# Strassen products for query and key, and PSUM banks of their own for turned tiles, in a kernel of retention, channel MLP and mixture of attention experts

## The chip, the cores and the metric

The kernel runs on one core of a Trainium2 chip. The metric is the device time of one execution in microseconds (us), the median of several runs. Matmuls run on TensorE (PE; its loads of weights are listed as PEld), elementwise work on VectorE (DVE), ScalarE (ACT) and GpSimd (POOL); SyncE (SP) issues all transfers. All inputs and outputs are fp32, and matmuls of large operands are made from a rounded high part and a low part (three matmuls: high x high, high x low, low x high).

## The reference, cut to what matters

```python
# 1 retention: B=2, H=8, S=768, D=64
for t in range(S):
    state = gamma * state + einsum('bhd,bhe->bhde', k[:, :, t], v[:, :, t])
    y[:, :, t] = scale * einsum('bhd,bhde->bhe', q[:, :, t], state)
x = y as [B, S, 512]
# 2 channel MLP, d = 512, inner 2048
xn = (x - mean) / sqrt(var + 1e-6) * g_ln
x = x + maximum(xn @ w_ch1, 0) @ w_ch2
# 3 mixture of 4 attention experts, head size 64, the best 2 of each token
logits = x @ w_gate ; w = softmax of the two best
for e in range(4):
    q, k, v = x @ wq[e], x @ wk[e], x @ wv[e]
    a = softmax(causal(q @ k.T / 8))
    out += w[e] * (a @ v @ wo[e])     # where e is among the two best
```

## The kernel before, in words

The work is written down as steps (`P.add`): each names the engines that may do it with a planned cost, the buffers that it reads and writes, and a priority (its place in the program, a bias, and a rank from the table `RANK`, which is kept by step name). `Plan.issue` then runs a simulation in Python: whenever an engine is free it takes the ready step of the lowest priority whose buffers find a place, and the order found is the order in which the instructions are issued. At run time every engine works through its own list in that order; a planned time that is not kept turns into a wait. Loads are planned at 372 GB/s and a latency of 2.2 us, and all go through SP's queue in order.

SBUF is one arena with places given by kind (`PL`), PSUM is eight banks of 512 words. Turned tiles (transposes on PE) go to places of kind `pb` (in the retention) and `pc` (in the attention). A turned tile has two halves, one for each half of the partitions, and `two` puts them at the same columns of two neighbouring banks; two such tiles of 256 columns share a pair of banks. The planner takes them for independent.

Stage 1, `r_tile`, 12 times (6 chunks of 128 tokens x 2 batches): keys and queries (`kq`) and values and keys (`vk`) are loaded, four and three buffers; scores (L581), masking (DVE L587), the chunk's own part (L610), the part from the state (L600), the update of the state (L618); then the tile is turned (`turn`, L422, xT into t1), normalized (statistics L642 to L644, L650, L651, xn at L655), turned back (xn into t2), copied (xc, L664) and split into a high and a low part, XH and XL.

Stage 2 is the MLP in eight slices f of 256 inner columns. Weights arrive in pieces (`load_piece`, `split_piece` on ACT, POOL and DVE). For f = 0 and 1 the first product is plain (`m_h`, L766). For the other six it is a Strassen scheme of seven products in place of eight (`m_h7`, L858) with sums of tokens (`x_sums`, POOL, once per batch) and of weights (`w_sums`). The second product, `m_c` (L788), is added to the running state XT by DVE; for f = 7 the sum is split again into XH and XL (L798, L801, L804). XT itself is not kept then.

Stage 3: `q_proj` makes queries and keys of one token half and one half of the columns with 12 matmuls (L952); `q_val` makes values and gate logits (L976); `a_scores` makes scores, softmax and scaling by the gate (L1047, L1054, L1062, L1068, L1069, L1076); `a_turn` turns the probabilities in parts of up to four blocks (L422) and copies them out on ACT or DVE (`COPY`, L446); `a_value` (L1117) and `a_out` (L1144) follow. Batch 1's projections are mixed with batch 0's attention. The groups of two query tiles are taken in the order 1, 2, 0 in batch 0 and 0, 1, 2 in batch 1. At the start some matmuls on constants (L529) keep PE at work until data is there.

Of the kernel before, what the change touches and what calls it, by code (L numbers as in the profile page):

```python
# [19 lines left out]
try:  # L20
# [15 lines left out]
E, HD = 4, 64  # L36
# [12 lines left out]
SWITCH = 0.125  # L49
LAST = 10000  # L50
FILL = 12
TWO = ("pb", "pc")
# [6 lines left out]
WORDS = 205 * KB  # L59
QUEUES = {"ps1": "s", "ps2": "s", "pr": "pr", "pt": "pt", "ptn": "pt", "sm": "sm", "at": "at", "w": "w", "h": "h", "raw": "raw", "wy": "wy",  # L60
          "w1": "w1", "S": "S", "t": "t", "u": "u", "sf": "sf",
          "am": "am", "vs": "vs", "xn": "xn", "xc": "xc"}
ROUNDED = {"x", "w", "w1", "S", "t", "h", "wq", "wk", "wv", "wo", "qk0", "qk1", "at"}


class Buf:
# [1249 lines left out]
```

## Time and profile before

| | us |
|---|---|
| median of 3 runs (442.19 to 445.38) | 442.72 |
| the profiled execution | 442.45 |
| its span in the trace | 440.7 |
| busy: PE, PEld | 429.4, 402.4 |
| busy: DVE, ACT, POOL | 309.8, 217.7, 212.0 |
| share of PE in the chain that ended last | 90% |

The span runs from the first to the last instruction of the trace. Busy time of an engine is the union of its instructions. The chain that ended last is followed back from the last instruction, at each step to what released it. The idle time before a group is given with the releasers, the instructions whose end let it start.

### The profile page before, as it was taken

The numbers are of one execution on the slowest core, as the hardware profiler recorded it, in microseconds if no ns is written. First come the engines' busy times: TensorE is split into PE (matmuls) and PEld (weight loads), VectorE is DVE, ScalarE is ACT, GpSimd is POOL, SyncE is SP. The second block draws the span as 40 slices with busy tenths as digits, with TensorE's granted clock in tenths as the row PEclk, the third lists the DMA queues.
The fourth block names the chain that finished last, engine by engine and source line by source line (L and its number), as shares of the span: only waits on it lengthen the run. The fifth ranks groups of instructions, "written<-read, shape, count | busy, mean of one in ns | idle before, by whom it ended". The sixth has DMA issues, their size and how long they took to land.

```text
span 440.7 us, 9076 instructions
## 1 busy us (share of the span) xinstructions
PE 429.4 (97%) x3546; PEld 402.4 (91%) x3546; DVE 309.8 (70%) x743; ACT 217.7 (49%) x460; POOL 212.0 (48%) x219
## 2 busy tenths in 40 slices
PE   9988999999999999999999999999999999999996
PEld 8877889999999999999999999999999877887765
DVE  2769978765778876868877655668556778667663
ACT  1568775342656346335353264234533666656552
POOL 2668865999999528117136054200401343422430
PEclk9999999999999999999999999999999999999999
DMA  8999432210322304104112002001100001001121
GB/s 288 328 337 345 133 109 84 97 49 1 106 86 92 101 0 143 50 1 136 54 59 88 1 1 96 1 0 55 48 1 1 1 12 39 2 0 49 50 97 49
DMA packets 11995, 35.18 MB, mean 80 GB/s; under 512 B 1840, under 2 KB 2480, under 8 KB 11952
## 3 DMA queue, kind: packets, MB, share of 16 engines
q1 hardware_dynamic: 11952, 34.60, 22.7%
q8 instruction: 28, 0.46, 0.4%
q14 instruction: 15, 0.12, 0.1%
HBM read 31.45 MB, written 3.15 MB: 79 GB/s over the span
## 4 chain that ended last, share of the span: by engine, by line
PE 90%; ACT 3%; DVE 2%; DMA 2%; POOL 1%; issue 1%; SPq 0%; POOLq 0%; DVEq 0%
PE ps L788 30%; PE ps L858 20%; PE ps L766 8%; PE ps L952 8%; PE ps L1117 4%; PE ps L976 4%; PE ps L422 4%; PE ps L1144 4%; PE ps L1047 3%; DMA raw<-in_w_dram 2%; PE ps L529 2%; PE ps L610 1%; PE ps L581 1%; ACT xn L655 1%; PE ps L600 1%
## 5 line engine op out<-in xcount | busy, mean ns | idle before, releaser
L788 PE MATMUL ps<-h,w 128*128 128x384 f32 x768 | 142.4, 335 | 0.0
L788 PEld LDWEIGHTS ps<-h,w 128*128 128x128 f32 x768 | 133.7, 188 | 0.7 <-DVE ps L798 0.3
L794 DVE TENSOR_TENSOR xT<-xT,ps 128x384 f32<-128x384 f32 x112 | 60.2, 550 | 30.6 <-PE ps L788 30.1
L1076 POOL TENSOR_SCALAR pr<-pr,sm,gate 128x384 f32<-128x384 f32 (+5 forms) x48 | 34.0, 718 | 77.9 <-DVE sm L1069 34.1
L719 POOL TENSOR_TENSOR w<-wy,w 128x512 fp32r<-128x512 f32 x26 | 34.0, 1319 | 38.1 <-PE ps L788 23.4
L858 PE MATMUL ps<-t,S 128*128 128x384 f32 x216 | 42.1, 334 | 0.0
L858 PEld LDWEIGHTS ps<-t,S 128*128 128x128 f32 x216 | 37.8, 188 | 0.0
L1062 ACT ACTIVATE pr<-pr,sm 128x384 f32<-128x384 f32 (+5 forms) x48 | 31.7, 663 | 9.9 <-DVE sm L1054 9.9
L766 PE MATMUL ps<-x,w 128*128 128x384 f32 x192 | 35.2, 337 | 0.0
L877 ACT ACTIVATE h<-ps 128x384 fp32r<-128x384 f32 x36 | 17.7, 490 | 32.9 <-PE ps L788 20.6
L766 PEld LDWEIGHTS ps<-x,w 128*128 128x128 f32 x192 | 33.2, 188 | 0.3
L685 ACT ACTIVATE wx<-raw 128x512 f32<-128x512 f32 x32 | 21.5, 671 | 23.8 <-DVE ps L692 16.0
L687 POOL TENSOR_SCALAR wx<-wx 128x512 f32<-128x512 f32 x32 | 20.0, 625 | 23.9 <-ACT wx L685 23.0
L867 ACT ACTIVATE u<-ps 128x384 f32<-128x384 f32 x36 | 17.5, 488 | 25.3 <-PE ps L858 16.6
L858 PE MATMUL ps<-x,w 128*128 128x384 f32 x144 | 28.6, 334 | 0.0
L689 DVE TENSOR_SCALAR ps<-wx 128x512 uint32<-128x512 uint32 x32 | 22.0, 688 | 6.4 <-POOL wx L687 6.1
L858 PEld LDWEIGHTS ps<-x,w 128*128 128x128 f32 x144 | 25.3, 188 | 0.0
L1054 DVE CUSTOM_DVE_ANT_0 pr<-ps,mask 128x384 f32<-128x384 f32 (+4 forms) x48 | 22.1, 495 | 3.2 <-PE ps L1047 2.2
L695 DVE SCALAR_TENSOR_TENSOR wy<-raw,ps 128x512 uint32<-128x512 uint32 x32 | 21.8, 683 | 2.3 <-POOL w L719 1.7
L879 DVE SCALAR_TENSOR_TENSOR h<-ps,h 128x384 fp32r<-128x384 f32 x36 | 19.4, 551 | 5.3 <-ACT h L877 5.2
L692 DVE SCALAR_TENSOR_TENSOR ps<-wx,ps 128x512 uint32<-128x512 uint32 x32 | 22.2, 695 | 1.1
L587 DVE TENSOR_TENSOR am<-ps,caus 128x512 f32<-128x512 f32 x24 | 15.5, 683 | 9.9 <-PE ps L581 9.9
(122 smaller groups left out, 822.7 us busy)
## 6 DMA issues: line engine op xcount, KB each, us to landing
raw<-in_w_dram SPq DMA_DIRECT2D x32, 512.0 KB, 3.4
kq<-in_kq_dram SPq DMA_DIRECT2D x11, 512.0 KB, 5.1
vk<-in_vk_dram SPq DMA_DIRECT2D x9, 512.0 KB, 5.5
out_dram<-ob SPq DMA_DIRECT2D x11, 256.0 KB, 2.0
vk<-in_vk_dram SPq DMA_DIRECT2D x4, 256.0 KB, 3.8
vraw<-in_wv_dram SPq DMA_DIRECT2D x1, 520.0 KB, 3.9
kq<-in_kq_dram SPq DMA_DIRECT2D x2, 256.0 KB, 5.2
mraw<-in_wk_dram SPq DMA_DIRECT2D x1, 512.0 KB, 4.6
```

The source lines that it names most:

```text
L689: DVE(0.69, lambda: dve.tensor_scalar(u32(z), u32(x), 4, 1, op0=OP.logical_shift_left, op1=OP.logical_shift_right), r=[x], w=[z])
L692: DVE(0.7, lambda: dve.scalar_tensor_tensor(u32(z), u32(x), 0x80000000, u32(z), op0=OP.bitwise_and, op1=OP.bitwise_or), r=[x, z], w=[z])
L695: DVE(0.7, lambda: dve.scalar_tensor_tensor(u32(y), words(0), 29, u32(z), op0=OP.logical_shift_right, op1=OP.bitwise_or), r=[raw, z], w=[y])
L719: POOL(1.3, lambda: pool.tensor_tensor(f32r(l), f32(y), f32(h), OP.subtract), r=[y, h], w=[l])
L766: pe.matmul(f32(pa, TB), lhsT=wt, rhs=blk(f32r(xt[b][j]))[:, k], start=(n == 0), stop=(n == 11))
L788: pe.matmul(f32(pa, TB), lhsT=wt, rhs=t, start=(n == 0), stop=(n == 5))
L794: DVE(0.55, lambda: dve.tensor_tensor(blk(f32(xt))[:, k], blk(f32(xt))[:, k], f32(pa, TB), OP.add), r=[pa] + [(xt, cc, w) for cc in range( ...
L858: pe.matmul(f32(pa, TB), lhsT=wt, rhs=t, start=(first and n == 0), stop=(n == 5), skip_group_check=True)
L952: pe.matmul(f32(pa, TB), lhsT=mw(n, lo, k, p * 128, (p + 1) * 128), rhs=blk(f32r(xt))[:, k], start=(i == 0), stop=(i == 11))
L1054: DVE(0.22 + wide * 1.04e-3, lambda ks=ks, n=n, z=z, SC=SC: dve.tensor_tensor_reduce(f32(PR[z])[:, ks], f32(SC[z])[:, :wide], f32(MASK)[:, ...
L1062: ACT(act_c(nk) + .18, lambda pr=pr, z=z: act.activation(f32(pr, nk), f32(pr, nk), AF.Exp, bias=f32(sm)[:, z:z + 1], scale=-1.0, accum_out ...
L1076: POOL(0.34 + nk * 0.84e-3, lambda pr=pr, z=z, e=e: pool.tensor_scalar(f32(pr, nk), f32(pr, nk), f32(sm)[:, 6 + z:7 + z], GT[b, j][:, cc, ...
```

## The change

- Query and key projections: `q_proj` now takes a whole batch and one weight and makes seven products of six matmuls in place of eight. The sums of wk and wq are made when these are loaded (`load_mw` 4 to 6). The sums of tokens are made by a second `x_sums` per batch, from XT, which the last `m_c` now writes as well (`m_c` 5, an ACT copy). Value projections of a batch come ahead of its query and key projections.
- Turned tiles: each has a pair of banks of its own; three places for `pb`, four for `pc`. Scores and outputs may use every bank. The third group of a batch is turned in two parts of up to six blocks, not three of up to four, and the value product waits only for the parts that it reads.
- The sum c22 of `m_h7` goes to PSUM; the sums of weights are made by POOL alone.
- 14 KB more of SBUF for each partition: six places for `kq`, four for `vk`, and more for turned probabilities; `pr` has 11 places in place of 12.
- The planner: transfers at 335 GB/s; an engine is free for its next step 0.05 to 0.1 us ahead of a step's end (`LEAD`); the two batches' states count as one buffer. The table of ranks is new throughout and is left out here.

```diff
--- before.py
+++ after.py
...
+LEAD = {"V": 0.085, "A": 0.1, "G": 0.05}
...
-TWO = ("pb", "pc")
...
-WORDS = 205 * KB
+WORDS = 219 * KB
...
+        n.eng = {e: c - LEAD.get(e, 0.0) for e, c in eng.items()}
...
+        n.lat = lat + max(LEAD.get(e, 0.0) for e in eng)
...
+    PL["kq"] += region(o_z, 4 * KB, 2)
+    PL["vk"] += region(o_z + 8 * KB, 4 * KB, 1)
...
+    PL["Sq"] = region(o_z, 4 * KB, 2) + region(o_h + 28 * KB, 4 * KB, 2)
+    PL["uq"] = region(o_z + 8 * KB, 3 * KB // 2, 4)
...
-    PL["pr"] = region(o_xt, 3 * KB, 8) + region(o_h + 24 * KB, 3 * KB, 4)
...
+    PL["pr"] = region(o_xt, 3 * KB, 6) + region(o_r + 36 * KB, 3 * KB, 4) + region(o_h + 24 * KB, 3 * KB, 1)
...
-    PL["psa"] = banks[4:][::-1]
-    PL["ps1"] = banks[:4]
+    PL["psa"] = banks[::-1]
+    PL["ps1"] = banks
...
-    PL["pb"] = [("P", 1024 * i + 256 * k, 256) for i in (1, 2, 3) for k in range(2)]
-    PL["pc"] = [("P", 1024 * i + 256 * k, 256) for i in (3, 2) for k in range(2)]
...
-    def two(b):
-        i, k = divmod(b.at[1], 1024)
-        return ps[:, 1024 * i:1024 * i + 1024].rearrange("p (h c) -> p h c", h=2)[:, :, k:k + 256]
+    PL["pb"] = [("P", 1024 * i, 1024) for i in (1, 2, 3)]
+    PL["pc"] = [("P", 1024 * i, 1024) for i in (3, 2, 1, 0)]
...
-        P.add({"D": nbytes / 372e3 + 0.03}, lambda e: fn(), r, w, lat=2.2)
+        P.add({"D": nbytes / 335e3 + 0.03}, lambda e: fn(), r, w, lat=2.2)
...
-            PE(0.47, upd, form="columns", r=[(vk, 1), vs] + (["first"] if i == 1 else []), w=[(STATE, b)] + (["first"] if i == 0 else []))
+            PE(0.47, upd, form="columns", r=[(vk, 1), vs], w=[STATE])
...
-            P.add({"V": 1.5, "G": 0.76} if f < ALONE else {"G": 0.75}, lambda e, i=i, p=p, q=q, op=op: (dve if e == "V" else pool).tensor_tensor(
+            P.add({"G": 0.75}, lambda e, i=i, p=p, q=q, op=op: (dve if e == "V" else pool).tensor_tensor(
...
-        P.add({"V": 2.4, "G": 2.41} if f < ALONE else {"G": 2.5}, lambda e: (dve if e == "V" else pool).tensor_tensor(f32r(l), f32(t), f32(h), OP.subtract),
+        P.add({"G": 2.5}, lambda e: (dve if e == "V" else pool).tensor_tensor(f32r(l), f32(t), f32(h), OP.subtract),
...
+        ACT(0.49, lambda: act.activation(blk(f32(xt))[:, k], f32(pa, TB), AF.Copy), r=[pa], w=[(xt, "k", k)])
+        P.at = "m_c 6"
         DVE(0.55, lambda: dve.tensor_tensor(blk(f32r(xl))[:, k], f32(pa, TB), blk(f32(xh))[:, k], OP.subtract),
-            r=[pa, (xh, "k", k)], w=[(xl, "k", k)] + (keys(xl) if k == 0 else []))
...
+    def x_sums(b, own=True):
...
-        for t, kh, j in ((2, 0, 1), (0, 0, 0), (1, 1, 1), (3, 1, 0)):
+        for t, kh, j in ((2, 0, 1), (0, 0, 0), (1, 1, 1), (3, 1, 0)) if own else ():
...
-            both(lambda en, t=t, p=p, q=q: en.tensor_tensor(plain(tl[t]), plain(tl[p]), plain(tl[q]), OP.subtract),
-                 [tl[p], tl[q]], [tl[t]])
+            both(lambda en, t=t, xp=xp, xq=xq: en.tensor_tensor(plain(tl[t]), xp(), xq(), OP.subtract), rp + rq, [tl[t]])
...
-        c22 = new("u")
+        c22 = new("ps")
...
+        if n in ("wk", "wq"):
+            sh, sl = new("Sq"), new("Sq")
...
+            for i, p, q, op in ((0, lambda: at(0, 1), lambda: at(1, 1), OP.add),
+                                (1, lambda: part(0), lambda: at(0, 0), OP.subtract),
+                                (2, lambda: at(0, 0), lambda: at(0, 1), OP.subtract),
+                                (3, lambda: at(1, 0), lambda: part(1), OP.subtract)):
+                P.at = "load_mw 4"
+                POOL(0.76, lambda i=i, p=p, q=q, op=op: pool.tensor_tensor(part(i), p(), q(), op), r=[raw], w=[sl])
+            P.at = "load_mw 5"
+            ACT(1.1, lambda: act.activation(f32r(sh), plain(sl), AF.Copy), r=[sl], w=[sh])
+            P.at = "load_mw 6"
+            POOL(2.41, lambda: pool.tensor_tensor(f32r(sl), plain(sl), f32(sh), OP.subtract), r=[sl, sh], w=[sl])
+            MW[n, "S"] = (sh, sl)
...
-    def q_proj(b, j, n, p):
...
+    def q_proj(b, n):
+        sh, sl = MW[n, "S"]
...
+        def product(pa, wn, xn, first):
...
-            PE(1.06, mm, r=list(MW[n][:2]) + xkeys(xh) + xkeys(xl) + ["seven"], w=[pa])
...
+            PE(1.04, mm, r=[h, l] + xr + ["seven"], w=[pa])
...
+        def add(dst, pa, u):
+            P.at = "q_proj 3"
+            DVE(0.55, lambda: dve.tensor_tensor(f32(dst, TB), f32(pa, TB), f32(u), OP.add), r=[pa, u], w=[dst])
...
+        pa, pb, pc = (new("ps") for _ in range(3))
+        product(pa, "a0", "x00", True)
+        c1 = keep(pa)
+        product(pb, "s1", "t1", True)
+        add(pb, pb, c1)
+        product(pa, "y0", "x10", False)
+        out(pa, 0, 0)
+        u2 = keep(pb)
+        product(pc, "s0", "t0", True)
+        product(pb, "s2", "t2", False)
+        u3 = keep(pb)
+        c22 = new("ps")
+        add(c22, pc, u3)
+        product(pb, "y1", "t3", False)
+        out(pb, 1, 0)
+        product(pc, "s3", "x11", False)
+        add(pc, pc, u2)
+        out(pc, 0, 1)
+        out(c22, 1, 1)
...
+            for z in range(2):
+                dve.tensor_scalar(m[:, 4 + z:5 + z], m[:, 2 + z:3 + z], 1e-9, None, op0=OP.add)
...
-            for s0 in range(0, len(slots), 4):
-                part = slots[s0:s0 + 4]
+            half = (len(slots) + 1) // 2 if len(slots) > 4 else len(slots)
+            for s0 in range(0, len(slots), half):
+                part = slots[s0:s0 + half]
...
+        half = (0, 4, 6)[g]
+        needs = {j0: sorted({min((2 * j0 + i) // half, 1) if half else 0 for i in (0, 3)}) for j0 in range(0, nj, 2)}
...
+    x_sums(0, False)
     flush()
+    x_sums(1, False)
...
     def q_phase(b):
         q_alloc(b)
         for j in range(NB):
-            for n in ("wk", "wq"):
-                for p in range(2):
-                    q_proj(b, j, n, p)
-            P.bias += 20 * (b + 1)
             for t in range(TPB):
                 q_val(b, TPB * j + t)
             gates(b, j)
-            P.bias -= 20 * (b + 1)
+        for n in ("wk", "wq"):
+            q_proj(b, n)
...
```

## Rows read from the trace of the kernel before

**Rows 1.** Stages: span, busy us (instructions) of PE, PEld, DVE, ACT, POOL; clock, DMA, GB/s.

```profile
0.00:45.00 45.00, 40.05 (x700) 35.17 (x702) 29.55 (x72) 23.56 (x50) 25.86 (x38) 1.00 0.91 321
80.00:120.00 40.00, 40.00 (x233) 40.00 (x232) 26.94 (x45) 16.72 (x30) 39.75 (x29) 1.00 0.17 61
82.90:319.00 236.10, 236.10 (x1362) 235.67 (x1360) 169.47 (x305) 105.75 (x200) 123.80 (x101) 1.00 0.17 57
319.00:440.70 121.70, 115.38 (x1113) 96.66 (x1112) 79.80 (x302) 63.22 (x166) 33.99 (x48) 1.00 0.08 27
```

**Rows 2.** Chain of work that ended last: start us, us, what.

```profile
7.05 2.02 PE ps L581 x32
...
48.18 1.99 PE ps L581 x32
...
82.86 8.33 PE ps L788 x48
...
306.65 8.32 PE ps L952 x48
314.97 4.16 PE ps L788 x24
...
319.86 1.24 PE ps L788 x6
...
325.26 8.60 PE ps L976 x72
```

**Rows 3.** Groups of PE, 0 to 82.86 us: busy, mean ns | idle before, releasers.

```profile
L529 PE MATMUL ps<-negs 128*128 128x128 f32 x32 | 6.7, 396 | 1.1 <-DVE half L546 1.1
...
L422 PE MATMUL ps<-ident,xn 64*128 64x64 f32 x96 | 5.6, 231 | 1.2 <-ACT xc L664 0.6 <-DVE mv L642 0.4
L422 PE MATMUL ps<-ident,xT 64*128 64x64 f32 x96 | 5.2, 231 | 1.9 <-ACT xn L655 1.2 <-ACT xc L664 0.6
```

**Rows 4.** The same chain, one landing of weights.

```profile
20.52 7.56 DMA raw<-in_w_dram
```

**Rows 5.** Waits of SP's queue: us in total, times, longest.

```profile
SPq L505 <- PE ps L618: 12.8, 6, 3.7
```

**Rows 6.** Waits of all engines: us in total, times, longest.

```profile
DVE pt L446 <- ACT pt L446: 4.0, 8, 1.2
```

**Rows 7.** Groups of PE, 319 to 440.7 us.

```profile
L422 PE MATMUL ps<-ident,pr 64*128 64x64 f32 x336 | 15.8, 228 | 2.8 <-DVE pt L446 1.6 <-ACT ptn L446 0.7 <-DVE at L1131 0.3
```

**Rows 8.** The chain again, turns of 16 and 6.

```profile
371.74 0.66 PE ps L422 x16
...
425.87 0.33 PE ps L422 x6
```

**Rows 9.** Timeline of PE: start us, us, what.

```profile
20.01 0.46 PE L422 MATMUL ps<-ident,xT 64*128 64x64 f32 x8
20.31 0.41 PE L422 MATMUL ps<-ident,xn 64*128 64x64 f32 x8
...
34.74 0.41 PE L422 MATMUL ps<-ident,xT 64*128 64x64 f32 x8
```

**Rows 10.** Timeline of ACT.

```profile
21.69 0.60 ACT L664 ACTIVATE xc<-ps 128x512 f32<-128x512 f32 x1 [1.46 <-POOL vs L571]
...
23.05 0.78 ACT L655 ACTIVATE xn<-ps,mv 128x512 f32<-128x512 f32 x1
...
41.07 0.78 ACT L655 ACTIVATE xn<-ps,mv 128x512 f32<-128x512 f32 x1 [1.80 <-POOL mv L651]
```

**Rows 11.** Groups of POOL, shapes apart.

```profile
L821 POOL TENSOR_TENSOR t<-t,t 128x768 f32<-128x768 f32 x8 | 15.0, 1876 | 0.3
...
L735 POOL TENSOR_TENSOR sf<-wy 128x256 f32<-128x256 f32 x6 | 4.7, 778 | 0.0
...
L925 POOL TENSOR_TENSOR wv<-vraw,wv 128x1040 fp32r<-128x1040 f32 x1 | 2.4, 2443 | 0.1
```

**Rows 12.** Timeline of DVE.

```profile
307.17 1.94 DVE L804 TENSOR_TENSOR x<-ps,x 128x384 fp32r<-128x384 f32 x4
```

More of the change, by code (lines that the diff above doesn't have):

```diff
@@ L218, in fits @@
                 for o in live.get(sp, ()):
-                    if (o.users or o.end > t) and any(x < y + size and y < x + o.at[2] for x in strips(o.kind, o.at[1])
-                                                      for y in strips(b.kind, off)):
+                    if (o.users or o.end > t) and o.at[1] < off + size and off < o.at[1] + o.at[2]:
                         break
@@ L421, in turn @@
                 hs = slice(64 * h, 64 * h + 64)
-                pe.transpose(two(dst)[:, h, i * 64:i * 64 + 64], src(i)[hs], ident[hs, hs])
+                pe.transpose(two(dst, 64 * n)[:, h, i * 64:i * 64 + 64], src(i)[hs], ident[hs, hs])
     P = Plan()
@@ L818, in x_sums, with part @@
                  keys(XH[b][j]) + keys(XL[b][j]), [tl[t]])
-        for t, p, q in ((0, 2, 0), (2, 1, 2), (1, 1, 0), (3, 3, 1)):
+        xs = {2: (0, 1), 0: (0, 0), 1: (1, 1), 3: (1, 0)}
+        def part(t, new):
+            if own or new:
+                return lambda: plain(tl[t]), [tl[t]]
+            kh, j = xs[t]
+            return lambda: f32(XT[b][j])[:, kh * TW:(kh + 1) * TW], [(XT[b][j], "k", 2 * kh + k) for k in range(2)]
+        for t, p, q, made in ((0, 2, 0, ()), (2, 1, 2, ()), (1, 1, 0, (0,)), (3, 3, 1, (1,))):
+            (xp, rp), (xq, rq) = part(p, p in made), part(q, q in made)
             P.at = "x_sums 2"
-            both(lambda en, t=t, p=p, q=q: en.tensor_tensor(plain(tl[t]), plain(tl[p]), plain(tl[q]), OP.subtract),
-                 [tl[p], tl[q]], [tl[t]])
+            both(lambda en, t=t, xp=xp, xq=xq: en.tensor_tensor(plain(tl[t]), xp(), xq(), OP.subtract), rp + rq, [tl[t]])
         for t in range(4):
@@ L941, in q_alloc, with mm @@
             VV[b, t] = new(f"vv{b}")
-    def q_proj(b, j, n, p):
-        cs = slice(j * TB, (j + 1) * TB)
-        pa = new("ps")
-        xh, xl = XH[b][j], XL[b][j]
-        for hf in range(2):
-            def mm(hf=hf):
-                i = 6 * hf
-                for k in (2 * hf, 2 * hf + 1):
-                    for lo, xt in ((0, xh), (0, xl), (1, xh)):
-                        pe.matmul(f32(pa, TB), lhsT=mw(n, lo, k, p * 128, (p + 1) * 128), rhs=blk(f32r(xt))[:, k],
-                                  start=(i == 0), stop=(i == 11))
+    def q_proj(b, n):
+        sh, sl = MW[n, "S"]
+        def product(pa, wn, xn, first):
+            h, l = (sh, sl) if wn[0] == "s" else MW[n][:2]
+            c0, step = (256 * int(wn[1]), 128) if wn[0] == "s" else ((512 if wn[0] == "y" else 0) + 128 * int(wn[1]), 256)
+            if xn[0] == "t":
+                xs = TH[b][int(xn[1])], TL[b][int(xn[1])]
+                xr, xat = list(xs), lambda k: tuple(f32r(t)[:, k * TB:(k + 1) * TB] for t in xs)
+            else:
+                kh, xs = int(xn[1]), (XH[b][int(xn[2])], XL[b][int(xn[2])])
+                xr, xat = xkeys(xs[0]) + xkeys(xs[1]), lambda k: tuple(blk(f32r(t))[:, 2 * kh + k] for t in xs)
+            def mm():
+                i = 0
+                for k in range(2):
+                    wh, wl = (f32r(t)[:, c0 + k * step:c0 + k * step + 128] for t in (h, l))
+                    xh, xl = xat(k)
+                    for wt, t in ((wh, xh), (wh, xl), (wl, xh)):
+                        pe.matmul(f32(pa, TB), lhsT=wt, rhs=t, start=(first and i == 0), stop=(i == 5), skip_group_check=True)
@@ L954, in mm @@
                         i += 1
             P.at = "q_proj 1"
-            PE(1.06, mm, r=list(MW[n][:2]) + xkeys(xh) + xkeys(xl) + ["seven"], w=[pa])
-        hi, lo = (QK[n, y, b, p] for y in range(2))
-        by = 0.125 if n == "wq" else 1.0
-        P.at = "q_proj 2"
-        ACT(0.485, lambda: act.activation(f32r(hi)[:, cs], f32(pa, TB), AF.Copy, scale=by), r=[pa], w=[(hi, j)])
-        P.at = "q_proj 3"
-        DVE(0.556, lambda: dve.scalar_tensor_tensor(f32r(lo)[:, cs], f32(pa, TB), by, f32(hi)[:, cs], op0=OP.mult, op1=OP.subtract),
-            r=[pa, (hi, j)], w=[(lo, j)])
+            PE(1.04, mm, r=[h, l] + xr + ["seven"], w=[pa])
@@ new lines, in keep, with out @@
+        def keep(pa):
+            u = new("uq")
+            P.at = "q_proj 2"
+            ACT(0.49, lambda: act.activation(f32(u), f32(pa, TB), AF.Copy), r=[pa], w=[u])
+            return u
+        def add(dst, pa, u):
+            P.at = "q_proj 3"
+            DVE(0.55, lambda: dve.tensor_tensor(f32(dst, TB), f32(pa, TB), f32(u), OP.add), r=[pa, u], w=[dst])
+        def out(src, p, j):
+            cs = slice(j * TB, (j + 1) * TB)
+            hi, lo = (QK[n, y, b, p] for y in range(2))
+            by = 0.125 if n == "wq" else 1.0
+            P.at = "q_proj 4"
+            ACT(0.485, lambda: act.activation(f32r(hi)[:, cs], f32(src, TB), AF.Copy, scale=by), r=[src], w=[(hi, j)])
+            P.at = "q_proj 5"
+            DVE(0.556, lambda: dve.scalar_tensor_tensor(f32r(lo)[:, cs], f32(src, TB), by, f32(hi)[:, cs], op0=OP.mult, op1=OP.subtract),
+                r=[src, (hi, j)], w=[(lo, j)])
@@ L1099, in a_turn @@
                 COPY(n * C, lambda pt=pt, s0=s0, n=n: f32(pt)[:, s0 * C:(s0 + n) * C].rearrange("p (n h c) -> p h n c", n=n, h=2),
-                     lambda pa=pa, n=n: two(pa)[:, :, :n * 64].rearrange("p h (n c) -> p h n c", n=n),
-                     [pa], [(pt, s0 // 4)])
+                     lambda pa=pa, n=n: two(pa, n * 64).rearrange("p h (n c) -> p h n c", n=n),
+                     [pa], [(pt, s0 // half)])
         return PT
@@ L1122, in a_value @@
                 PE((0.87 if j0 + 2 < nj else 0.65) * len(zs) / 2, mm, form="columns",
-                   r=[VV[b, j0], VV[b, j0 + 1]] + [(pt, j0 // 2) for pt in (*PT, *also)], w=[av])
+                   r=[VV[b, j0], VV[b, j0 + 1]] + [(pt, i) for pt in (*PT, *also) for i in needs[j0]], w=[av])
             cs = slice(zs[0] * C, (zs[-1] + 1) * C)
```

38 lines of the change are left out of this document (19 added, 19 removed), and 148 rows, old and new, of the table RANK.

## Prediction

> **What bounds the kernel now.** I read the busy time by stage first, then the chain of work that ended last, then the idle time of TensorE (PE) by group, then the other engines where the change puts work. In [rows 1] PE is busy for all of 82.9 to 319 us, at a granted clock of 1.00; it has idle time only in the first 45 us and after 319. DVE, ACT and POOL have time left in each of these stages; POOL alone is full for one stretch, 39.75 of 40 us from 80 to 120. So between 82.9 and 319 nothing but fewer or shorter matmuls shortens the run. The chain gives their price: 48 matmuls of 384 columns take 8.33 us [rows 2], 0.1735 us each, 1.04 us for a product of six.
>
> PE's idle time is small and countable. In the first 45 us it is busy for 40.05 [rows 1], so 4.95 us are idle; 1.1 us of that is ahead of the filler matmuls of L529, which nothing can use because the first keys land at 7.05 [rows 2, 3]. Of the fillers' 6.7 us, 28 of 32 run before 7.05 and four (0.64 us) after. What can be won there is 4.95 - 1.1 + 0.64 = 4.5 us. After 319 PE is busy for 115.38 of 121.70 us [rows 1]; of the 6.3 idle 2.8 us lie in front of the turns of the probabilities at L422 [rows 7], and the other 3.5 I put behind the last matmul (last copy and store). That is all: 4.5 and 2.8 us of stalls, and the matmuls themselves.
>
> **The sum goes against the profiled execution**, 442.45 us (span 440.7 and 1.75 around it), which is 0.27 under the median of 442.72.
>
> **Strassen for query and key.** Before, each of two batches, two token halves, two weights and two column halves takes 12 matmuls, 192 in all. After, each batch and weight takes seven products of six, 2 x 2 x 7 x 6 = 168. The operands keep their shapes (128 x 128 weights, 384 columns), and the 48 matmuls of L952 in [rows 2] take 8.32 us, the same price as in the channel MLP. 24 x 0.1735 = 4.16 us leave PE, in a stretch where PE has no idle to swallow them. What is added lies on other engines: per weight four sums and a low part on POOL, per batch eight POOL operations of 1.88 us [rows 11] for the sums of tokens, with four ACT copies, 16 ACT copies of the final state (m_c 5), and three ACT copies and three DVE additions per batch and weight. From 82.9 to 319 POOL is busy for 124 of 236 us, and after that for 34 of 121.7 [rows 1]: 2 x 5.5 us for the weights (0.78 a sum, 2.4 a low part [rows 11]) and 2 x 15 us for the tokens fit. Cost on PE: nothing, if the sums come in time, which I check with the numbers of the path. The last DVE low part of batch 0 ends at 307.17 + 1.94 = 309.1 [rows 12]; add 0.5 for the new copy, 2.4 for the low part of wv, which POOL must make first [rows 11], 8 x 1.88 and one ACT copy of about 0.8: the last sum is there at 327.9. PE at 306.65 still has five products of the MLP (30 matmuls of L788, 5.2 us), then value projection of batch 0, 8.6 us [rows 2], then four products that can run without sums of tokens (a0 and y0 for each weight; s3 must follow s0 in its bank), 4.2 us: 324.6. The last sum, t3, is used after three other products if the weights go one after the other, after six if they interleave: at 327.7 or 330.9, against 327.9. So 0 to 3.0 us of cover are left in batch 0; batch 1 has the attention of batch 0 as cover. I take 0.2 for it; beyond that each us that POOL is late is one on PE.
>
> **Turned tiles with banks of their own.** Before, two turned tiles share a pair of banks. The waits show what that does: DVE's copy of one part waits for ACT's copy of another, eight times, 4.0 us [rows 6]. The two parts share no column. PE is hit where its next turn needs the bank. In the first stage all 3.1 us of idle time before L422 name xn, xc or mv [rows 3], so the bank is a part of the 4.5 us above. Not all of it is the bank. The chain shows another cause: a load of MLP weights takes 7.56 us to land at 20.52 [rows 4], where the planner reckons 512 KB / 372 GB/s + 2.2 = 3.6 us; ACT's queue stands behind it, and xn after that. SP in turn stands 12.8 us for a free place of vk [rows 5]. The change speaks to each: own pairs, transfers planned at 335 GB/s (the mean over the first 45 us is 321, [rows 1]) and six and four places for kq and vk in place of four and three. But the DMA engines are 0.91 busy in this stage [rows 1], so the last load cannot come much earlier. Bounds: 0 to 4.5 us gained; I take 2.0, a little under half, since latencies and loads remain. In attention: 0 to 2.8 us [rows 7]; I take half, 1.4, since the next true dependency (the softmax, the copy itself) comes right behind the false one.
>
> The batch's third group is turned in two parts in place of three, eight turns and eight copies fewer. A run of 16 transposes takes 0.66 us and one of 6 takes 0.33 [rows 8], 0.033 per transpose and 0.13 fixed. Eight times 0.13 is 1.0 us if each stood alone; many run back to back, so 0 to 1.0, and I take 0.5.
>
> **Edits with one answer.** c22 in PSUM holds one of eight banks more until its two outputs are made, 12 times; PE is busy there without a gap [rows 1], and products of other quarters and of m_c stand between, so 0, at worst one product (1.04 us) each time. Refined waits of the value product and the planner's lead times change only the order: 0, and they are in the bounds of the stalls above. Five sums of weights go from DVE to POOL, 0.78 us each [rows 11], 3.9 us in or just behind the stretch where POOL is full; PE holds first-kind MLP work against it, so 0, at worst 3.9. One more small DVE instruction in each softmax, and m_c 6 that waits for one more ACT copy: 0.2 to 0.5 us per chain, beside PE work; I take 0.3 in all for the chains at the end.
>
> Sum: 442.45 - 4.16 - 2.0 - 1.4 - 0.5 + 0.2 + 0.3 = 434.9.
>
> **The price of own banks.** A pair now holds one turned tile. xT is held from 20.01 to 23.83 in one tile and from 34.74 to 41.85 in another, xn from 20.31 to 22.29 [rows 9, 10]: 5.8 to 9.1 us of a pair for each token tile. Twelve tiles have their scores between 7.05 and 50.2 [rows 2], 3.6 us each. On three pairs the need is 1.9 to 3.0 us, which fits; on two (single banks for scores, outputs and weight splits keep the third) it is 2.9 to 4.6, which may not. The Trainium skill, TensorEngine Tiling (Array Packing), section Gotcha 1: PSUM Pressure, says that different row tiles write to different PSUM banks and so use more of them; by that the sum would lose its 2.0 us and pay the price of the second rival below, and no row of the kernel before decides it.
>
> **The rivals.** First, the stalls only move: the bank is not what PE waits for, but the loads and the softmax behind it. For it: 0.91 of DMA busy and the 7.56 us landing. Against: eight waits of parts that share no column. Then Strassen alone stands, 442.45 - 4.16 = 438.3, with 437.5 to 441 around it for small new waits.
>
> Second, slower: places for turned tiles decide the first stage. In-order PE stands before a turn until a pair is free. At 4.55 us (9.1 over two pairs) in place of 3.6 it loses 0.95 us for each of six tiles (until the first MLP half is ready as other work) to twelve: 5.7 to 11.4 us. Time: 434.9 + 2.0 + 5.7 to 11.4 = 442.6 to 448.3, about 445. It makes the kernel slower than before from (442.7 - 436.9) / 12 = 0.5 us a tile over all twelve, a pace over 4.1. For it: the one tile held 7.1 us. Against: on three pairs even that tile fits.
>
> Third, POOL is late with the sums of tokens, since in batch 1 they share its queue with the 48 scalings of probabilities: if it loses 5 us, 2 to 5 pass the cover: 437 to 440, and 439 to 445 if both batches lose.
>
> Fourth, better: with loads planned at the true rate nearly all stalls go, 442.45 - 4.16 - 4.5 - 2.8 - 1.0 = 430.0.
>
> **How the numbers follow.** The forecast (432 to 437.5) has 0.47, the better case 0.08, stalls that move 0.24, the places 0.12, late sums 0.09. One per cent, about what a measurement of this kernel can tell from no change, is 4.4 us: faster is under 438.3, slower over 447.1. Faster: 0.47 + 0.08 + a quarter of 0.24 + a little of the late sums = 0.62. Slower: the upper half of the places and the tail of two causes together, 0.08. Same: 0.30. The range 430.5 to 441.0 leaves out nearly all of the places, most of the late sums and the end of the better case, together 0.2.
>
> **What would show it.** Right: 168 matmuls in the query and key projection at 0.1735 us each; PE without a gap between its last MLP product and the first products on sums; the waits of DVE on ACT at the copies of turned parts gone or under 1 us; idle time ahead of turns in the first 45 us halved; loads of weights landing about when ACT reaches them. Wrong: PE idle before L422 or before scores with a copy of an older turned tile as releaser (second rival); PE idle before the products on t, with POOL as releaser (third); the chain in the first 45 us still made of landings, at the same total (first).

## The result, and the profile after

The changed kernel takes 445.64 us in the median (443.77 to 448.58), the kernel before 442.38 on the same chip: 1.0078 of it, with an interval of 1.0060 to 1.0096. It is slower by 0.8%, where 434.9 was forecast with a range of 430.5 to 441.0: outside the range, though within the one per cent that the prediction counts as no change. The profiled execution of the changed kernel took 445.14 us, with a span of 443.2. It is one of the shorter ones: its mean granted clock is 0.995, while 15 of the 20 executions have 0.988 to 0.992, and the seven at 0.988 or 0.989 took 446.3 to 448.6 us.

Lines of the changed kernel have moved: L422 of before is L430, L581 is L589, L618 is L626, L788 is L796, L952 is L995, L976 is L1051. Two rows of its page, in 40 slices of 11.1 us:

```profile
PE   8889999999999999999999999999995999999996
PEclk9999999999999999999999999999998999999999
```

Slice 31 (332 to 343 us) is half idle on TensorE (PE), with a lower clock; nothing in the kernel before looks like it. The same by stages (span, busy us of PE, PEld, DVE, ACT, POOL, clock, DMA share, GB/s), against [rows 1]:

```profile
0.00:45.00 45.00, 39.55 (x651) 34.31 (x652) 28.67 (x70) 20.96 (x41) 27.43 (x37) 1.00 0.86 303
45.00:118.80 73.80, 73.56 (x622) 69.35 (x621) 52.91 (x107) 38.97 (x71) 64.98 (x60) 1.00 0.27 88
118.80:313.70 194.90, 194.90 (x1124) 194.31 (x1123) 138.26 (x257) 96.14 (x187) 102.77 (x94) 1.00 0.18 60
313.70:335.60 21.90, 21.90 (x145) 21.62 (x143) 12.41 (x21) 13.21 (x25) 21.82 (x13) 1.00 0.01 4
335.60:345.50 9.90, 5.11 (x27) 4.97 (x26) 8.17 (x19) 2.72 (x7) 3.82 (x3) 0.83 0.00 1
```

The start is no better than before: 39.55 us busy of 45 against 40.05, with DMA at 0.86 and 303 GB/s against 0.91 and 321. The stage of the channel MLP is full, as before. Then POOL, idle or light there before, is full from 313.7 to 335.6 us, and right behind that PE is busy for 5.11 of 9.9 us. The chain of work that ended last, around that place (start us, us, what), against [rows 2]:

```profile
305.45 8.32 PE ps L796 x48
313.77 12.54 PE ps L995 x72
326.31 4.31 PE ps L1051 x36
331.18 1.20 DVE ga L1082
332.37 1.81 DVE ga L1083
...
337.83 1.62 DVE ga L1087
340.40 3.69 PE ps L995 x12
...
347.46 1.24 PE ps L995 x6
```

This chain splits the whole difference. The MLP is done at 313.77 with no projection made yet. Before, its last product ended at 321.10 (319.86 + 1.24 [rows 2]), with 8.32 us of projection and 0.72 us of attention scores made in between: 312.06 by the same count. So the first two stages lost 1.7 us, where 2.0 were to be won. From there to the end it was 440.7 - 312.06 = 128.6 us and is 443.2 - 313.77 = 129.4, where 5.6 us (4.16 + 1.4 + 0.5 - 0.2 - 0.3) were to go. The second loss has a name in the chain: five VectorE (DVE) instructions on tiles of 48 and 12 columns (all five stand in the next rows), 8.1 us together. The timeline shows what goes on beside them (DVE, then ACT, POOL and PE; in brackets the idle time before and who ended it):

```profile
331.18 1.20 DVE L1082 TENSOR_TENSOR ga<-ga 128x48 f32<-128x48 f32 x1
332.30 1.88 DVE L1083 TENSOR_TENSOR ga<-ga 128x48 f32<-128x48 f32 x1
334.21 1.76 DVE L1084 TENSOR_TENSOR ga<-ga,before 128x48 f32<-128x48 f32 x1
336.00 1.72 DVE L1085 TENSOR_TENSOR ga<-ga 128x48 f32<-128x48 f32 x1
337.65 0.15 DVE L1086 TENSOR_REDUCE ga<-ga 128x3 f32<-128x12 f32 x1
337.83 1.61 DVE L1087 TENSOR_TENSOR ga<-ga 128x12 f32<-128x12 f32 x1
...
339.48 0.21 ACT L1091 ACTIVATE ga<-ga 128x12 f32<-128x12 f32 x1 [6.30 <-DVE ga L1087]
...
330.46 1.85 POOL L840 TENSOR_TENSOR t<-xT 128x768 f32<-128x768 f32 x1
332.26 7.16 POOL L845 TENSOR_TENSOR t<-t,t 128x768 fp32r<-128x768 f32 x4
...
340.40 2.29 PE L995 MATMUL ps<-t,wq 128*128 128x384 f32 x6 [4.79 <-ACT uq L1003]
```

These are the gates of the first block of tokens. An instruction of the same line takes 206 ns in the median of four and 1876 ns here:

```profile
L1083 DVE TENSOR_TENSOR ga<-ga x4: 201/206/1876, 332.3 to 399.6; 128x48 f32<-128x48 f32 x4
```

In the kernel before, POOL stood idle beside the same gates (L1007 to L1012 there; the third is shown), and they took 0.17 to 0.21 us each:

```profile
316.96 0.63 POOL L1219 MEMSET mask<- 128x640 f32 x1
332.58 1.32 POOL L1076 TENSOR_SCALAR pr<-pr,sm,gate 128x384 f32<-128x384 f32 x2 [14.99 <-DVE gate L1026]
...
330.15 0.21 DVE L1009 TENSOR_TENSOR ga<-ga,before 128x48 f32<-128x48 f32 x1
```

The four held from 332.30 on end when an instruction of POOL ends: POOL's row of four from 332.26 puts their ends about 1.8 us apart, at 334.1, 335.9, 337.6 and 339.4, and DVE's at 334.2, 336.0, 337.7 and 339.4. One DVE instruction comes through between two of POOL's. The reduction of L1086, which reads one operand, takes 0.15 us in the middle of it. ACT waits 6.30 us for the gates; behind its exponential stand the copies of L1003 that empty PE's banks, and so PE stands 4.79 us. The matmuls that follow run at the lower clock: the granted clock is 0.83 in the mean from 335.6 to 345.5, part of that stretch at the lower of its two levels (1.2 and 2.4 GHz), after those 4.79 us of idleness, and the twelve of L995 take 3.69 us where twelve take 2.08. 4.79 + 1.61 = 6.4 us.

The Trainium skill has the rule: SBUF — State Buffer, section Who interferes with whom, says that a DVE instruction with two inputs in SBUF contends with a GpSimd instruction that reads SBUF, and that whoever comes second is blocked until the first is through. The trace agrees: 0.2 us become 1.6 to 1.9 with two inputs, and 0.15 us stay 0.15 with one.

The own banks did what they were to do. Groups of PE up to the end of the MLP (to 313.77 us; busy, mean ns | idle before, releasers), against [rows 3]:

```profile
L589 PE MATMUL ps<-kq 64*128 64x128 f32 x192 | 13.5, 282 | 0.8 <-DMA kq<-in_kq_dram 0.7 <-DVE wy L703 0.2
...
L626 PE MATMUL ps<-vs,vk 128*64 128x64 f32 x160 | 6.7, 226 | 1.7 <-POOL vs L579 1.7
...
L608 PE MATMUL ps<-kq,sn 64*64 64x128 f32 x160 | 6.7, 282 | 1.4 <-DMA kq<-in_kq_dram 0.7 <-DVE am L595 0.5
L430 PE MATMUL ps<-ident,xn 64*128 64x64 f32 x96 | 5.6, 233 | 0.7 <-ACT xn L663 0.7
L430 PE MATMUL ps<-ident,xT 64*128 64x64 f32 x96 | 5.1, 229 | 0.0
```

Idle time before turns fell from 3.1 us to 0.7. It came back before the scores (L589), the part from the state (L608) and the update of the state (L626): 0.8, 1.4 and 1.7 us, where the kernel before had 0.8 in all. SyncE (SP) shows one reason; its queue at the start, and one row of its waits (us in total, times, longest):

```profile
4.01 0.43 SPq L521 DMA_DIRECT2D tab<-in_tabY_dram  x1
6.77 0.33 SPq L503 DMA_DIRECT2D kq<-in_kq_dram  x1
7.14 0.43 SPq L508 DMA_DIRECT2D caus<-in_caus_dram  x1
...
SPq L503 <- PE ps L589: 3.0, 2, 2.2
```

From 4.44 to 6.77 us SP issues nothing: the second tile's kq waits for the score matmuls that read the first tile's. Kq has six places, and at that moment three of the first four had never been used; but the planner takes the first place of its list that it holds to be free, and in the plan that one is free at that time. All loads stand behind it, the causal table (caus) among them, on which DVE's first mask then waits until 11.59 us (8.20 before).

In attention, against [rows 7], the idle time before turns fell from 2.8 us to 0.7:

```profile
L430 PE MATMUL ps<-ident,pr 64*128 64x64 f32 x336 | 15.1, 228 | 0.7 <-DVE ga L1063 0.4 <-ACT ptn L454 0.2
```

### The profile page after: what moved, and what is told of

It reads as the page before. It is cut to its first block, busy times and chain, and to the rows that moved or that the text cites. A ratio compares the mean times of both kernels' runs of the same rounds, so it can differ in the third digit from the quotient of the medians.

```text
span 443.2 us, 9117 instructions
## 1 busy us (share of the span) xinstructions
PE 428.4 (97%) x3522; PEld 399.2 (90%) x3522; DVE 315.2 (71%) x772; ACT 231.3 (52%) x484; POOL 255.1 (58%) x252
## 4 chain that ended last, share of the span: by engine, by line
PE 80%; POOL 7%; DVE 6%; DMA 3%; issue 1%; ACT 1%; SPq 0%; POOLq 0%; ACTq 0%
PE ps L796 27%; PE ps L876 20%; PE ps L995 7%; PE ps L774 5%; PE ps L1196 5%; PE ps L1223 4%; PE ps L1122 4%; PE ps L430 3%; DMA vk<-in_vk_dram 3%; PE ps L1051 3%; POOL x L677 1%; PE ps L618 1%; POOL t L827 1%; POOL vs L579 1%; PE ps L589 1%
## 5 line engine op out<-in xcount | busy, mean ns | idle before, releaser
L796 PE MATMUL ps<-h,w 128*128 128x384 f32 x768 | 145.4, 335 | 0.0
L796 PEld LDWEIGHTS ps<-h,w 128*128 128x128 f32 x768 | 133.7, 188 | 0.9 <-DVE h L897 0.2
L802 DVE TENSOR_TENSOR xT<-xT,ps 128x384 f32<-128x384 f32 x112 | 61.6, 551 | 34.4 <-PE ps L796 34.0
L895 ACT ACTIVATE h<-ps 128x384 fp32r<-128x384 f32 x48 | 23.3, 489 | 26.5 <-PE ps L796 18.0
L897 DVE SCALAR_TENSOR_TENSOR h<-ps,h 128x384 fp32r<-128x384 f32 x48 | 26.3, 551 | 5.3 <-ACT h L895 5.1
L890 DVE TENSOR_TENSOR ps<-ps,u 128x384 f32<-128x384 f32 x36 | 20.3, 563 | 13.2 <-ACT u L885 10.7
L845 POOL TENSOR_TENSOR t<-t,t 128x768 fp32r<-128x768 f32 x16 | 29.2, 1847 | 0.3
```

What stands on the lines that cost most here:

```text
L796: pe.matmul(f32(pa, TB), lhsT=wt, rhs=t, start=(n == 0), stop=(n == 5))
L802: DVE(0.55, lambda: dve.tensor_tensor(blk(f32(xt))[:, k], blk(f32(xt))[:, k], f32(pa, TB), OP.add), r=[pa] + [(xt, cc, w) for cc in range( ...
L845: both(lambda en, t=t: en.tensor_tensor(f32r(tl[t]), plain(tl[t]), f32(th[t]), OP.subtract), [tl[t], th[t]], [tl[t]])
L895: ACT(0.49, lambda: act.activation(f32r(h, TB), f32(src, TB), AF.Relu), r=[src], w=[h])
L897: DVE(0.55, lambda: dve.scalar_tensor_tensor(f32r(l, TB), f32(src, TB), 0.0, f32(h, TB), op0=OP.max, op1=OP.subtract), r=[src, h], w=[l])
```

## The experiments

Each edits the changed kernel and leaves the order of its instructions as it was. All were timed in five rounds beside the kernel before; ratios are to that one, with their 95% intervals.

| kernel | median us | ratio to before |
|---|---|---|
| changed kernel | 445.64 | 1.0078 (1.0060 to 1.0096) |
| e1 gates write constants | 438.04 | 0.9885 (0.9857 to 0.9914) |
| e2 sums in halves | 442.65 | 0.9997 (0.9976 to 1.0018) |
| e3 table first | 445.76 | 1.0056 (1.0030 to 1.0081) |
| e4 sums in quarters, table first | 444.20 | 1.0031 (1.0009 to 1.0053) |
| e7 loads' places in turn | 444.20 | 1.0028 (1.0012 to 1.0044) |
| e9 gates' first part with one SBUF operand | 442.17 | 0.9988 (0.9970 to 1.0007) |
| e10 all places in turn | 444.21 | 1.0041 (1.0025 to 1.0056) |
| e11 = e9 + e10 | 440.46 | 0.9944 (0.9927 to 0.9961) |
| e14 all the gates with one SBUF operand | 438.72 | 0.9896 (0.9871 to 0.9921) |
| e12 = e7 + e14 | 437.81 | 0.9897 (0.9879 to 0.9915) |
| e13 = e12 + table first | 437.74 | 0.9896 (0.9876 to 0.9915) |

**Is it the second operand in SBUF?** e1 lets the gates' instructions read nothing:

```
-            dve.tensor_tensor(gt(), lf, le, OP.is_gt)
-            dve.tensor_tensor(eq(), lf, le, OP.is_equal)
+            dve.memset(gt(), 0.0)
+            dve.memset(eq(), 0.0)
...
-            dve.tensor_tensor(w(), lg(), mx()[:, :, None].to_broadcast([128, TPB, E]), OP.subtract)
+            dve.memset(w(), 0.0)
```

> In the changed kernel TensorE stands idle 4.79 us at 340.40, behind the gates of the first query block. Here the gates' VectorE instructions that read two operands from SBUF (is_gt, is_equal, the two that follow, the subtraction, the product by the weights and the last product) write constants instead and read nothing; their number, their order and the issue order of all else stay. Left out: the comparison of the gates' logits; every token takes all four experts at 0.25. Theory A (each of these instructions is held while GpSimd, which forms the second batch's x sums from SBUF, runs one of its 1.85 us instructions): the five instructions that now take 1.20 to 1.88 us take 0.1 to 0.25 us each, the idle of 4.79 us falls under 0.5 us, the granted clock stays at 1.00 there, and about 6.4 us go (4.79 and the 1.6 us of the slower matmuls behind): near 439.2 us, 0.993 of the kernel before. Rival B (GpSimd is late with the sums of tokens, and the gates only stand in line): the idle stays at 4 us or more, time near 445. Rival C (the idle is for places in PSUM, the gates being beside the path): the idle is at another instruction but no shorter, time 443 to 446.

Measured 438.04 us. The five instructions take 0.07 to 0.10 us, and PE has no idle time from 313.7 to 345.5:

```profile
331.35 0.10 DVE L1082 MEMSET ga<- 128x48 f32 x1
...
331.72 0.07 DVE L1087 MEMSET ga<- 128x12 f32 x1
...
335.60:345.50 9.90, 9.90 (x73) 1.00 0.00 1
```

Theory A holds, with a little more than the 6.4 us reckoned (7.6 between the medians, 443.2 - 436.6 = 6.6 between the spans). Rivals B and C fall. But e1 takes work away too (the comparison of the logits and what follows from it), so the next ones keep it.

**Does the length of POOL's instruction set the price?** e2 cuts it into two of 384 columns, e4 into four of 192 (the edit touches the sums of both batches, since both are formed by these lines):

```
+                for cs in pieces_of():
+                    en.tensor_tensor(plain(tl[t])[:, cs], xp()[:, cs], xq()[:, cs], OP.subtract)
```

> Each GpSimd subtraction of the second batch's x sums is issued as two of 384 columns, and its VectorE or ScalarE alternative likewise; nothing is left out. Theory A (a VectorE instruction with two SBUF operands is held until the running GpSimd instruction ends): the five gate instructions take about half, 0.7 to 1.0 us instead of 1.20 to 1.88, 8.2 us become about 4.5 us, TensorE's idle behind them falls from 4.79 us to about 1 us and the clock stays up: 440 to 441.5 us. Rival B (GpSimd's total work is what is late; halves add some overhead to it): no gain, 445 to 446.5 us. Rival D (the two engines share the port word by word, so that only total overlap counts and not the length of one instruction): the gate instructions keep 1.2 to 1.9 us, 445 us.

The held instructions take half; PE's idle time behind them is 0.71 and 1.53 us in place of 4.79, more than the 1 us expected, because DVE's own additions (L1016 here) stand behind the gates as well; the granted clock still falls, to 0.83 in the mean from 335.6 to 345.5:

```profile
331.44 1.05 DVE L1091 TENSOR_TENSOR ga<-ga 128x48 f32<-128x48 f32 x1
332.53 0.93 DVE L1092 TENSOR_TENSOR ga<-ga,before 128x48 f32<-128x48 f32 x1
333.50 0.94 DVE L1093 TENSOR_TENSOR ga<-ga 128x48 f32<-128x48 f32 x1
...
339.30 2.01 PE L1003 MATMUL ps<-x,Sq 128*128 128x384 f32 x6 [1.53 <-DVE ps L1016]
```

The time, 442.65, is 3.0 below the changed kernel and a little above the 440 to 441.5 expected. Rivals B and D fall: POOL does the same work in more instructions, and the hold is one instruction long.

**The table, and quarters.** e3 moves one transfer:

```
-                DMA(24e3, lambda: sp.dma_start(tabV, a["tabV"]), w=["tabV"])
+                def small():
+                    sp.dma_start(tabV, a["tabV"])
+                    sp.dma_start(caus, a["caus"])
+                DMA(24e3, small, w=["tabV"])
```

> The transfer of the causal table is issued with the table of values, ahead of the keys' and queries' loads, where the kernel before had it (it was issued at 7.14 us, with the first mask on VectorE at 11.59 us against 8.20 us before). Theory A: the first mask runs at 8 to 9 us, TensorE's useful work by 20 us rises from 9.6 us towards the 11.7 us of the kernel before, and 1 to 2 us go: 443.5 to 444.5 us, if GpSimd's chain from 76 to 94 us doesn't swallow it. Rival B (the start is bound by the bytes that TensorE needs, whatever their order: DMA moves 303 GB/s there): the next load is late instead, time 445 to 446 us. Rival C (the loss of the first stages lies behind 45 us, in GpSimd's part of the sums): useful work by 45 us rises by 1 us or more and the MLP still ends its 48 matmuls without a projection at 313.8 us.

> The GpSimd subtractions of the second batch's x sums in four parts of 192 columns each, and the causal table's transfer issued first; nothing is left out. Theory A for the gates: their five instructions take 0.4 to 0.6 us, TensorE's idle behind them is gone, and with the earlier table the time is 438 to 440 us, under the kernel before. If the gates' instructions are not held by the length of one GpSimd instruction: 444 to 446 us. If only the table's part fails: 439.5 to 440.5 us.

e3 gave nothing: the first mask began at 6.69 us, but its second half only at 13.97, behind kq; rival B holds, and the table's place was not the loss. In e4 the gates' instructions take 0.38 to 0.64 us, as theory A has it for quarters, yet the time is 444.2. The four quarters take 2.27 to 2.63 us where the whole took 1.8, and now PE waits for the sums of tokens, 2.4 us in three places, two of them shown; the second names an ACT copy that stands behind ACT's own wait of 2.12 us for such a sum:

```profile
315.40 1.68 PE L1006 MATMUL ps<-t,Sq 128*128 128x384 f32 x8 [0.55 <-POOL t L855]
321.49 2.38 PE L1006 MATMUL ps<-x,wk 128*128 128x384 f32 x12 [1.28 <-ACT uq L1014]
```

With the 0.8 us that PE still idles behind the gates that is 3.2 us, of the 4 to 6 by which the time lies over the expected 438 to 440; the rest is open. The expectation missed this. It is the third rival of the prediction (POOL late with the sums), which the changed kernel itself escapes: there PE has no idle time at all from 313.7 to 335.6.

**The place of a load.** e7 changes only which free place is taken:

```
-            for sp, off, size in b.places:
+            places = b.places
+            if b.kind in ("kq", "vk"):
+                places = sorted(places, key=lambda p: (p[1] >= 60 * KB, freed.get(p, 0.0)))
+            for sp, off, size in places:
```

> Only the choice among free places changes, for the keys-queries and values-keys loads: the place that has been free longest in the plan, not the first of the list. The order of all instructions stays. In the changed kernel the second tile's kq is put into the place of the first tile's kq, though three others were never used, and SyncE waits from 4.44 to 6.77 us for the score matmuls that read it, with every load behind it in its queue. Theory A (that wait, and others like it, are the loss of the first stage): SyncE issues that load by 5 us, DMA moves more than the 308 GB/s of 5 to 10 us (385 before), TensorE's useful work by 20 us rises from 9.6 us by 1 us or more, the 48 last matmuls of the MLP end 1 to 2.5 us earlier than 313.8, and the time is 443 to 444.5 us. Rival B (the start is bound by bytes, whatever the places): under 0.5 us, 445 to 446. Rival C (GpSimd's chain from 76 to 94 us takes back what the loads give): useful work by 45 us rises, the MLP still ends at 313.5 or later.

> As the kernel with loads' places in turn, but for all kinds of SBUF tiles for which it leaves the order of instructions as it is (masked scores, values, turned states, weights' rounded parts, sums, probabilities); PSUM stays. Theory A (the plan gives a place away as soon as it thinks it free, and the chip is later than the plan): beyond the loads' part another 0 to 1.5 us, 442 to 444 us. Rival B (places elsewhere are free long before): the same as with loads alone, within 0.5 us.

In e7 SP no longer stands before the second kq, and the MLP's last 48 matmuls, still in one piece, begin 2.1 us earlier (305.45 in the chain above):

```profile
4.47 0.43 SPq L508 DMA_DIRECT2D kq<-in_kq_dram  x1
4.95 0.43 SPq L513 DMA_DIRECT2D caus<-in_caus_dram  x1
...
303.33 8.32 PE ps L801 x48
```

From 10 to 20 us DMA moves 382 GB/s in place of 336. The median is 444.20, 1.4 us under the changed kernel, as theory A expected. The span is shorter by 1.4 us too, and not by 2.1. The trace shows why behind the gates: PE idles there as long as in the changed kernel (4.81 us), but the granted clock is then lower for longer, 0.66 in the mean from 335.6 to 345.5 against 0.83. e10, with nearly all SBUF tiles in turn, gives no more (444.21, clock 0.66 there as well): its rival B holds. The profiles of all kernels agree: the MLP's last product ends at 313.0 to 314.6 us in the seven with the places as they were (changed kernel, e1 to e4, e9, e14) and at 311.7 to 312.4 in the five with places in turn (e7, e10 to e13). And in the first 20 us the clock falls (0.91 in the mean) in three of the seven, e1, e3 and e9, in none of the five.

**The gates with the work kept.** e9 holds the logits and one mask in unused columns of a PSUM bank, so that no instruction of the first part reads two operands from SBUF (for the first batch; two instructions of the second's gates take 0.80 and 0.60 us beside POOL, and PE stands 0.35 us behind them); e14 does so for the second part too (the last two lines):

```
+            lz = lambda: ps[:, at:at + 12].rearrange("p (t e) -> p t e", e=E)
+            eq = lambda: ps[:, at + 12:at + 60].rearrange("p (t e f) -> p t e f", e=E, f=E)
...
+                dve.tensor_copy(lz(), lg())
+            lf = lz()[:, :, None, :].to_broadcast(sh)
...
+                rk = ps[:, 460:472].rearrange("p (t e) -> p t e", e=E)
+                sm = ps[:, 508:511]
```

> The first batch's gates compute the same, but the logits and the is_equal part are kept in 60 unused columns of a PSUM bank, so that none of the five instructions reads two operands from SBUF; one copy of 12 elements is added. Order and all else stay. Theory A (held by GpSimd for two SBUF operands): the five instructions take 0.15 to 0.35 us each, TensorE's idle of 4.79 us is gone, the time is 438 to 440 us, like the run with constants. Rival B (the constants took away something else: results that came too early, less work): they still take over 0.8 us each and the time stays over 443. Rival C (use of a bank that TensorE writes brings waits of its own): short instructions, but idle of over 1 us before a matmul or a gate instruction, 440 to 443.

> All places in turn and the first batch's gates with one operand in PSUM. If both causes are apart in time they add up: 6 to 7 us from the gates and 1 to 3 us from the places, 435.5 to 438.5 us, 0.984 to 0.991 of the kernel before. If the places give nothing: 438 to 439.5 us.

e9 took 442.17 us, and not the 438 to 440 of theory A. The first part's instructions do take 0.2 us, but the second part is now held in its turn:

```profile
334.10 0.81 DVE L1104 SCALAR_TENSOR_TENSOR gate<-ga 128x12 f32<-128x12 f32 x1 [0.28 <-ACT ga L1098]
...
335.14 1.57 DVE L1106 TENSOR_SCALAR ga<-ga 128x3 f32<-128x3 f32 x1
336.74 0.18 DVE L1107 RECIPROCAL ga<-ga 128x3 f32<-128x3 f32 x1
336.95 1.53 DVE L1108 TENSOR_TENSOR gate<-gate,ga 128x12 f32<-128x12 f32 x1
...
339.28 1.85 PE L995 MATMUL ps<-x,Sq 128*128 128x384 f32 x6 [1.85 <-DVE ps L1008]
```

PE's idle time falls to 1.85 us, and has another releaser, the addition queued on DVE behind the gates; the clock still falls (0.83 from 335.6 to 345.5). Rival C named this time, but not this cause: it is no wait for the bank. e11 adds the places in turn: 440.46, where 435.5 to 438.5 was expected, with the same 1.8 us of idle time. It is 1.7 us under e9, so the places show here too. The gates were only half mended, and e12 and e14 mend the rest.

> Loads' places in turn (only keys-queries and values-keys), and all instructions of the first batch's gates with at most one operand in SBUF: the ranks and the weights' sums lie in PSUM too, so that the last part of the gates, which in the kernel with one operand in PSUM still took 0.81, 1.57 and 1.53 us for three instructions and left TensorE idle for 1.85 us behind it, is no longer held by GpSimd either. Theory A: those three take 0.15 to 0.25 us, TensorE's idle there is under 0.3 us, the clock stays at 1.00 from 330 to 350 us, and 2 to 3 us more go than with places and the first part alone (440.46): 437 to 438.5 us. Rival B (the rest of the idle is the adds' own chain, VectorE after ScalarE): idle of 1 us or more remains, 439.5 to 440.5 us.

> As the kernel with loads' places in turn and all the gates, and the causal table's transfer issued with the table of values. With the places in turn the first mask on VectorE still began at 11.12 us, released by that table; here it should begin at 6 to 8.5 us. Theory A (with the wait for a place gone the table is what the first tiles stand for): TensorE's useful work by 20 us rises by 0.5 us or more and another 0.5 to 1 us goes, 436 to 437.5 us. Rival B (the table's place in the queue only moves the delay to the loads behind it, as when it was tried alone): within 0.4 us of the other kernel of this pair.

> The changed kernel with all instructions of the first batch's gates reading at most one operand from SBUF, the places of the loads as they were. It completes the square of gates and places. If the two causes are apart they add up: this kernel stands 1.4 us above the one with both (437.81), at 439.2 us within 0.7, and the gates alone are worth 6.4 us of 445.64. If the places' gain was only the room that the gates' stall left, or the other way round, it stands at 437.8 or above 440.

e12 took 437.81 us. The same instructions of the second part, POOL's row beside them, and PE's stretch behind them:

```profile
331.81 0.17 DVE L1112 SCALAR_TENSOR_TENSOR gate<-ps,ga 128x12 f32<-128x12 f32 x1 [0.22 <-ACT ga L1103]
...
332.23 0.17 DVE L1114 TENSOR_SCALAR ps<-ps 128x3 f32<-128x3 f32 x1
...
330.76 7.26 POOL L850 TENSOR_TENSOR t<-t,t 128x768 fp32r<-128x768 f32 x4
...
335.60:345.50 9.90, 9.90 (x73) 1.00 0.00 0
```

POOL works as before, and DVE's instructions are no longer held. PE runs without a gap and at full clock from 311 to 345.5. With e13 it is the best version here, faster than the kernel before by 1.0% (0.85 to 1.21%), and than the changed kernel by 1.8%. e13 equals it within 0.1 us: with the places mended the table's transfer is worth nothing either (rival B). e14, the gates alone, took 438.72, near the 439.2 of adding up; by ratios e12 and e14 can't be told apart, while the traces put the spans 2.2 us apart (435.6 and 437.8), all of it before the MLP's end (312.27 and 314.49); from there on both take 123.3 us, where the changed kernel takes 129.4. The execution of e14 that was profiled is the longest of its six (439.70; the shortest took 436.99), so 2.2 us is rather too much than too little. So the places' gain is shown by the medians of e7 and of e11 against e9 and by where the MLP ends in the traces; once the gates are mended, the medians (0.9 us apart) don't resolve it.

## Why the prediction was wrong

Against 434.9 the profiled execution is 10.2 us longer: 1.7 + 2.0 = 3.7 in the first two stages, 0.8 + 5.6 = 6.4 after them, and 0.2 around the span.

**The step that failed** stands in the part on Strassen: "What is added lies on other engines ... Cost on PE: nothing, if the sums come in time". The sums came in time; the third rival, which was to catch an error here, did not occur. What I left out is that POOL, forming the second batch's sums without a pause, holds other engines' short work: the gates' instructions on DVE went from 1.0 to 8.1 us, ACT's queue stood behind them, and PE behind ACT. I costed the added POOL instructions by POOL's free time alone (33.99 busy of 121.7 us [rows 1]) and never asked what DVE does beside them. e1, e2, e4, e9 and e14 show it: the price follows the length of POOL's instruction (DVE's take about 1.8, 0.94 and 0.5 us a piece beside wholes, halves and quarters) and is gone where no more than one operand is in SBUF.

**The first stage** was mis-sized by sign: -2.0 was taken and +1.7 came. PE's idle time at the turns did go with the shared bank (3.1 us became 0.7), though no run gives the turned tiles their own banks and nothing else. Wrong was that more places for kq and vk help by being there: the planner doesn't use them first, and SP's whole queue stood behind waits for places, one of them of 2.3 us at the very start (e7, which changes the places of all these loads: the MLP ends 2.1 us earlier). With that mended the MLP ends at 303.95 + 8.32 = 312.27 against 312.06 before: no gain and no loss, as the first rival (stalls only move) had it for this stage. The idle time on PE up to the MLP's end was 4.95 us before and 5.70 after (45 - 39.55, and 0.25 up to 118.8). The other 1.0 us of the loss lies in busy time: the same 2392 matmuls keep PE busy for 307.1 us before (312.06 - 4.95) and 308.1 after (313.77 - 5.70), at a granted clock of 1.00 in both, and for 307.2 in e7. Why is open; the order of steps and loads is new too (the table of ranks), and no run tries it apart.

**Strassen** was right in the count and in part in the price: there are 168 matmuls, and 72 of them, in one row, take 12.54 us, 0.174 each. But most of the others run in sixes between other products, and there six take 1.24 us in the chain above and not 1.04. In e12, without the stall at the gates, all 168 keep PE busy for 32.6 us, the 192 before for 35.1: 2.5 us less, where 4.16 were reckoned. **Attention turns and the eight turns fewer** gave more than was taken: the idle time before turns fell by 2.1 us (1.4 taken), the turns' busy time by 0.7 (15.8 to 15.1; 0.5 taken). In sum the part after the MLP is 435.6 - 312.27 = 123.3 us in e12 against 128.6, 5.3 less where 5.6 were reckoned. That the sum comes so near is luck in part, since its terms miss in opposite directions. The terms put at nothing for c22 and for the sums of weights held: PE has 0.2 us of idle time from 45 to 313.7. **The price of own banks** (second rival) did not show: no idle time of PE names a copy of an older turned tile in the first stage. POOL's cover in batch 0, for which 0.2 us was taken, cost nothing, for another reason than the one worked out: POOL began the sums at 302.5, made the low part of wv after them and not before, and ended the last sum at 322.0 us, not at 327.9. e4 shows how thin that cover is: half a us more per sum, and PE idles 2.4 us.

With both causes mended the forecast is missed by 2.9 us (437.81 against 434.9): the first stage's 2.0 that did not come make up most of it.

## What to carry to other kernels

Work moved to an engine with free time is not free if its instructions hold up short work of another engine that lies on the path, as POOL's did with DVE's here: look for instructions of DVE with two SBUF operands beside back-to-back GpSimd instructions, and give one operand a place in PSUM, or make GpSimd's instructions shorter (each further piece cost 0.1 to 0.3 us in e2 and e4). When a planner picks places by first fit on its own clock, new places can stay unused while a load waits for the last reader of an old one; taking the place that had been free longest cost nothing in e7. A term won from stalls should be split by who else is due at that moment before half of it is booked.

## What the hardware showed that I had not expected

A DVE instruction of 12 to 48 columns with both operands in SBUF lasts as long as the rest of POOL's running instruction (0.2 us alone; in a row of them 1.6 to 1.9 beside instructions of 1.85 us, 0.93 to 1.05 beside halves), and only one comes through between two of POOL's. It also holds for a TENSOR_SCALAR of three elements with one SBUF operand (1.57 us from SBUF to SBUF in e9, 0.17 in PSUM beside the same POOL work in e12), but not for a reduction or a reciprocal from SBUF (0.15 to 0.18 us beside the same POOL instructions). The Trainium skill, SBUF — State Buffer, section Who interferes with whom, counts tensor_scalar among those that can take DVE's second port with one operand, and the reduction among those that never do; these rows agree.
